# The gate's depthwise convolution of a Branchformer layer, forward and gradient: from diagonal products on TensorE to products and sums on VectorE

## The chip, the core and the metric

The kernel runs on one core of one Trainium2 chip. Its engines work side by side and wait for each other by semaphores: PE (TensorE, matmuls into PSUM), DVE (VectorE), ACT (ScalarE), POOL (GpSimd), and SP (SyncE), which issues most of the DMAs. The metric is the device time of one execution in microseconds. Before the change it is 1294.91 us, the median of three runs (1287.72, 1295.05, 1294.91).

## What is computed

The reference is a layer of the Branchformer kind, forward and all gradients, for x of 2 x 4000 tokens of 144 channels, in bf16. The part that matters here is the local branch ("gate"), and its gradient:

```python
h = _gelu(jnp.einsum('btd,de->bte', xc, w_mlp_in))
u, g = (h[..., :D].copy(), h[..., D:].copy())
g = _layernorm(g, axis=-1)
gp = jnp.pad(g, ((0, 0), (pad, pad), (0, 0)))
gc = jnp.zeros_like(g)
for i in range(K):
    gc = gc + gp[:, i:i + T, :] * dw_csgu[i][None, None, :]
loc = jnp.einsum('btd,de->bte', u * gc, w_mlp_out)
```

So `gc` is a convolution over time with 5 taps, each channel by itself (depthwise). The gradient with regard to `g` is the same convolution with the taps in reverse order, applied to the gradient of `gc`; the gradient with regard to the taps `dw_csgu` (5 x 144) is a sum over all tokens of products of `g`, shifted by the tap, with the gradient of `gc`. Beside this branch stands attention over 4000 tokens (scores, softmax, values, and their gradients), and behind both a merging convolution with products.

## The kernel before: how the work is tiled and ordered

**Layout.** The 4000 tokens of a batch lie on 125 partitions (`PB`) with 32 consecutive tokens (`NB`) each: token t is partition t // 32, block t % 32. A shift in time by one token is therefore another block of the same partition; only at the first and last blocks does it come from the neighbouring partition (a DMA shifted by one partition).

**The attention loop** (`phase_att`, L1201) takes 64 steps, one for each block of 125 tokens of both batches, with a few more to drain. In each step PE computes four pairs of score and gradient products into PSUM (`quad`, L1273), DVE takes the scores out with a minimum (`S_min`, L1298), ACT takes the exponentials (L1304), the gradient's products are multiplied with the probabilities (`PdP`, L1310: an ACT copy and a DVE product in SBUF, or a direct DVE product from PSUM, L1312, for the last of the four), SP issues DMA transposes of the result, and PE multiplies the results with tokens (`Y_half`, `Z_half`, `X_group`). DVE adds the groups of `X` to an accumulator (L1416); the first group of each block is copied (L1414).

**The local units** (`local_units`, L546) are spread over the steps 2 to 26 for batch 0 and 34 to 60 for batch 1. They come in 16 units for a batch, of two blocks (`G2`) each. For unit g: two matmuls for the hidden layer (L590), the gelu and its derivative on ACT, DVE and POOL (L592 to L651), statistics (L610), the product of `go` with the merging weights (`dug_unit`, L618), the normalized gate (`e_gn`, L632, POOL) and the gradient of `gc` (`e_dgc`, L636, DVE). The last two are written side by side into a tile of a small ring, `gd`, `[125, 2, 2 blocks, 144]`.

**The convolution before** runs on PE. `t_unit` (L653) transposes both halves of a `gd` tile with four matmuls against the identity (channels 0 to 127) and four more for the 16 remaining channels, whose 5 taps are stacked on 80 partitions (`rem`); ACT copies the results (`gT`, `gS`). `gc_unit` (L671) multiplies for each block five shifted transposed tiles with diagonal matrices of the taps (`W.dgf`), and one stacked tile with `W.dgs`: 12 matmuls a unit, whose result ACT copies from PSUM (L678). `dgn_unit` (L686) does the same for the gradient with `W.dgm`, which has one column more: it gives the sum over the channels, which the gradient of the normalization needs. DVE reads this result from PSUM (L696, L700, L708). `dwc_unit` (L728) computes the gradient of the taps on PE, for every second unit: for channels 0 to 127 as products of all channel pairs whose diagonal `Final.dwc` (L1890) takes at the end, for the other 16 with the stacked tile.

**The order.** The program is written as one list, and `Planner.plan` (L927) then orders the instructions of each engine with a list scheduler: it has a cost for each instruction (`cost`, L891), a model of the DMA queue, the tiles' dependencies, and a table of lead times (`LEAD`, L792) that moves groups of instructions ahead or back. Each engine works strictly in that order. A round of the local branch (`round_`, L761) puts the new work of unit n beside the convolution of an older unit o.

**The head.** Before the loop, weights are loaded and prepared (`Head`, L116); PE runs 100 matmuls on zeros (`WARM`, L541; `warm`, L180) that the planner puts wherever PE has nothing else, and `conv` (L285) builds the diagonal matrices on POOL.

## Time and profile before

| | |
|---|---|
| median of three runs | 1294.91 us |
| the profiled execution | 1292.98 us |
| its span, first to last instruction | 1291.2 us |
| PE busy / weight loads | 1257.1 / 1040.6 us |
| DVE, ACT, POOL busy | 1047.1, 788.2, 501.1 us |
| instructions | 39494 |
| DMA | 185.80 MB, 76.7% of 16 engines' span on the main queue |
| granted TensorE clock, mean | 0.991 |

A time line or a group of the profile names the source line, the engine, the operation, output and inputs with their sizes, and the duration. The idle time behind it is that of the engine just before the instruction, with what ended it. Busy times of an engine are the union of its records, so two records that overlap count once. `PEclk` or the seventh figure of a window row is the share of the full TensorE clock that was granted. The record of a short matmul (0.22 us) is its latency; the next one starts much earlier, so what a matmul costs is read from start to start.

### The profile page before, as it was taken

To read this page: it belongs to the slowest core of one execution; us is meant where nothing else is said; L and a number is where in the kernel's file an instruction comes from. 1 tells how busy PE (TensorE), PEld (TensorE's weight loads), DVE (VectorE), ACT (ScalarE), POOL (GpSimd) and SP (SyncE) were. 2 spreads that over 40 slices of the span, in tenths; PEclk is the share of its full clock that TensorE was granted. 3 is DMA by queue.
4 is the path that set the end of the run, shared out by engine and by line. 5 is a ranking of instruction groups with operands and counts; after the bars stand their busy time and mean duration, and the time that the engine had idled before them with its cause. 6 is when DMAs were issued, how large, how long until landed. Compare 5 with 4: busy or idle time off the path is not lost.

```text
span 1291.2 us, 39494 instructions
## 1 busy us (share of the span) xinstructions
PE 1257.1 (97%) x15974; PEld 1040.6 (81%) x15974; DVE 1047.1 (81%) x2809; ACT 788.2 (61%) x1291; POOL 501.1 (39%) x976
## 2 busy tenths in 40 slices
PE   8999999999999999899899999999999999899898
PEld 6578888888888887777678888888888888799897
DVE  6589888988888887898888888899889887666925
ACT  4776666666665666556656666667566665435561
POOL 6265335444443434232444434444443433132410
PEclk8899999999999999999999999999999999999999
DMA  4477888888888888889898898887778788959611
GB/s 126 94 141 136 155 144 152 143 145 150 137 151 142 145 143 162 158 145 174 168 155 148 133 149 135 151 137 146 137 142 154 136 155 167 188 123 208 186 44 50
DMA packets 628829, 185.80 MB, mean 144 GB/s; under 512 B 604215, under 2 KB 623065, under 8 KB 628625
## 3 DMA queue, kind: packets, MB, share of 16 engines
q1 hardware_dynamic: 627506, 181.88, 76.7%
q8 instruction: 125, 2.05, 0.6%
q0 software_dynamic: 592, 1.18, 0.3%
q14 instruction: 58, 0.48, 0.1%
q10 hardware_dynamic: 548, 0.21, 0.1%
HBM read 22.96 MB, written 16.69 MB: 31 GB/s over the span
## 4 chain that ended last, share of the span: by engine, by line
PE 83%; DMA 6%; DVE 3%; ACT 3%; SPq 2%; POOL 1%; issue 1%; ACTq 0%; POOLq 0%
PE X L1410 20%; PE ps L1276 15%; PE yz L1363 10%; PE yz L1325 9%; PE ps L1283 7%; DMA ST<-Sbuf 2%; PE po L1783 2%; DMA PT<-Pbuf 2%; PE pd L625 1%; PE pd L692 1%; PE pc L677 1%; PE pj L1249 1%; PE Hps L1698 1%; PE pt L1265 1%; PE pw L737 1%; DVE Pbuf L1298 1%
## 5 line engine op out<-in xcount | busy, mean ns | idle before, releaser
L1298 DVE TENSOR_SCALAR_CACHE_REDUCE Pbuf<-ps 125x1000 bf16<-125x1000 f32 x256 | 306.4, 1197 | 93.9 <-PE ps L1283 90.0
L1304 ACT ACTIVATE Pbuf<-Pbuf,nm 125x1000 bf16<-125x1000 bf16 x256 | 278.6, 1130 | 91.1 <-DVE nm L1300 90.7
L1410 PE MATMUL X<-QBs,Sbuf 125*125 125x144 bf16 x2048 | 298.8, 229 | 0.8 <-DVE acc L1414 0.4
L1410 PE MATMUL X<-QBs,Pbuf 125*125 125x144 bf16 x2048 | 292.3, 226 | 0.0
L1410 PEld LDWEIGHTS <-Sbuf 125*125 125x125 bf16 x2048 | 259.3, 137 | 26.0 <-issue 25.8
L1314 ACT CAST Sbuf<-ps 125x1000 bf16<-125x1000 f32 x190 | 188.7, 993 | 132.4 <-PE ps L1283 131.1
L1276 PE MATMUL ps<-xaT_m,qt 128*125 128x500 bf16 x1024 | 263.7, 378 | 2.9 <-DVE Pbuf L1298 2.1
L1410 PEld LDWEIGHTS <-Pbuf 125*125 125x125 bf16 x2048 | 260.6, 137 | 0.9 <-issue 0.9
L1416 DVE TENSOR_TENSOR acc<-X,acc 125x432 f32<-125x432 f32 (+1 forms) x373 | 200.5, 549 | 25.2 <-PE X L1410 22.3
L1363 PE MATMUL yz<-xa_aug,ST 125*125 125x144 bf16 x2048 | 150.6, 228 | 6.1 <-DMA ST<-Sbuf 4.8
L1276 PEld LDWEIGHTS <-qt 128*125 128x125 bf16 x1024 | 121.5, 137 | 42.8 <-issue 4.6
L1325 PE MATMUL yz<-xa_aug,PT 125*125 125x145 bf16 x2048 | 146.1, 228 | 6.5 <-DMA PT<-Pbuf 6.5
L1363 PEld LDWEIGHTS <-ST 125*125 125x125 bf16 x2048 | 139.4, 138 | 9.9 <-DMA ST<-Sbuf 6.1
L1325 PEld LDWEIGHTS <-PT 125*125 125x125 bf16 x2048 | 137.4, 137 | 9.6 <-DMA PT<-Pbuf 7.4
L1316 DVE TENSOR_TENSOR Sbuf<-Sbuf,Pbuf 125x1024 bf16<-125x1024 bf16 x190 | 134.6, 710 | 3.5 <-ACT Sbuf L1314 3.1
L1283 PEld LDWEIGHTS <-qt 16*125 16x125 bf16 x1024 | 36.6, 128 | 101.2 <-issue 101.2
L1283 PE MATMUL ps<-XR,qt 16*125 16x500 bf16 x1016 | 111.1, 420 | 0.0
L1343 POOL TENSOR_SCALAR QBs<-qb,rl 125x144 bf16<-125x144 bf16 x64 | 27.0, 422 | 180.5 <-DVE rl L1331 151.1
L1312 DVE TENSOR_TENSOR Sbuf<-ps,Pbuf 125x1000 bf16<-125x1000 f32 x66 | 78.8, 1194 | 6.7 <-PE ps L1283 6.2
L720 POOL TENSOR_TENSOR A_dwc<-l_fl,A_dwc 128x512 f32<-128x512 f32 (+2 forms) x48 | 37.0, 771 | 78.8 <-ACT l_fl L719 78.8
L1267 ACT COPY qt<-pt 128x500 bf16<-128x500 bf16 x62 | 35.9, 578 | 45.5 <-PE pt L1265 44.8
L595 POOL TENSOR_SCALAR l_a<-l_sq 125x576 bf16<-125x576 bf16 x32 | 22.5, 702 | 101.6 <-ACT l_sq L593 101.3
(576 smaller groups left out, 2411.3 us busy)
## 6 DMA issues: line engine op xcount, KB each, us to landing
Yn_d<-yn SPq DMA_DIRECT2D x64, 35.2 KB
Zn_d<-zn SPq DMA_DIRECT2D x64, 35.2 KB
ug_d<-ugr SPq DMA_DIRECT2D x32, 70.3 KB
PT<-Pbuf SPq DMA_TRANSPOSE x126
ST<-Sbuf SPq DMA_TRANSPOSE x126
Yg<-Yn_d SPq DMA_DIRECT2D x8, 252.0 KB
go_h<-in_grad_out_dram SPq DMA_DIRECT2D x8, 252.0 KB
Yg<-ug_d SPq DMA_DIRECT2D x8, 252.0 KB
```

The source lines that it names most:

```text
L720: nc.gpsimd.tensor_tensor(acc, fl[0:rows, 0:n], acc, op=ALU.add)
L1276: mm = nc.tensor.matmul(pp[r // 2][:, r % 2, 0:CH], QT[i][:, 3 * h, :], bs(i)[0].xaT_m[:, c * CH:(c + 1) * CH], start=True, stop=False)
L1283: nc.tensor.matmul(pp[r // 2][:, r % 2, 0:CH], QT[i][rs, 1 + (q // 2 + h) % 2, :], xr, start=False, stop=True)
L1298: nc.vector.tensor_scalar(pv(Pbuf, i % NPB, c2), src, -1.0, 3.0e38, op0=ALU.mult, op1=ALU.min, accum_out=NM[i][:, c2:c2 + 1])
L1304: nc.scalar.activation(v, v, ACT.Exp, bias=NM[i][:, 4:5], scale=-1.0)
L1312: nc.vector.tensor_tensor(pv(Sbuf, i % NDB, c2), src, pv(Pbuf, i % NPB, c2), op=ALU.mult)
L1314: nc.scalar.copy(pv(Sbuf, i % NDB, c2), src)
L1316: nc.vector.tensor_tensor(sc, sc, pchunk(i % NPB, c2), op=ALU.mult)
L1325: nc.tensor.matmul(Y, PT[0:PB, j, 0:PB], S.xa_aug[:, j, 0:D + 1], start=(j == 0), stop=(j == NB - 1))
L1363: nc.tensor.matmul(Z, ST[0:PB, j, 0:PB], S.xa_aug[:, j, 0:D], start=(j == 0), stop=(j == NB - 1))
L1410: nc.tensor.matmul(X[:, jj, :], l, r, start=(n_ == 0), stop=(n_ == len(ops) - 1))
L1416: nc.vector.tensor_tensor(av, X[:, 0:nj, :], av, op=ALU.add)
```

## The change

The taps are no longer applied on PE. The two halves (normalized gate, gradient of `gc`) of all units are written into one ring `[125, 2, 16 blocks, 144]`: 12 blocks are in turn, and the first four are copied behind the twelfth, so that any window of five blocks is contiguous. The halves of the batch's edges wait in `hold` and are copied into the ring after round 13. The taps lie in SBUF on every partition (`W.Wc`, by one broadcast DMA; the second half is the reverse order, by a POOL copy). DVE multiplies, for each block, five blocks x 144 channels with five taps in one instruction, and sums the five products with three instructions a unit:

```diff
-    def t_unit(c, g):
-        pt = ps_w.tile([128, 8, 128], BF, tag="w")
...
+    def taps(g, a):
+        p = (G2 * g) % 12
+        for bi in range(G2):
+            nc.vector.tensor_tensor(prod[:, bi].rearrange("p a b -> p (a b)"), ring[:, a, p + bi:p + bi + 5, :].rearrange("p a b -> p (a b)"), W.Wc[0:PB, a, :], op=ALU.mult)
+        nc.vector.tensor_tensor(t2[:], prod[:, :, 0:2, :], prod[:, :, 2:4, :], op=ALU.add)
+        nc.vector.tensor_tensor(t1[:], t2[:, :, 0, :], t2[:, :, 1, :], op=ALU.add)
 
     def gc_unit(g):
-        pc = ps_w.tile([PB, G2, D], F32, tag="w")
-        for bi in range(G2):
-            i = G2 * g + bi
-            nc.tensor.matmul(pc[:, bi, :], gS[g % 2][:, bi, :], W.dgs[:, 0, 0:D], start=True, stop=False)
-            for kk in range(5):
-                nc.tensor.matmul(pc[:, bi, 0:128], col(0, i + kk), W.dgf[:, kk, :], start=False, stop=(kk == 4))
-        nc.scalar.copy(gc[:], pc[:])
+        taps(g, 0)
+        nc.vector.tensor_tensor(gc[:], t1[:], prod[:, :, 4, :], op=ALU.add)
...
     def dgn_unit(g):
-        pd = ps_w.tile([PB, G2, D + 1], F32, tag="w")
...
+        taps(g, 1)
+        rs, t = rsr[slot(g)], gd(g)
+        s1 = sm.tile([PB, G2], F32, tag="s1")
         s2 = sm.tile([PB, G2], F32, tag="s2")
         for bi in range(G2):
-            nc.vector.scalar_tensor_tensor(gc[:, bi, :], pd[:, bi, 1:D + 1], -1.0 / D, t[:, 0, bi, :], op0=ALU.mult, op1=ALU.mult, accum_out=s2[:, bi:bi + 1])
+            nc.vector.scalar_tensor_tensor(dgn[:, bi, :], t1[:, bi, :], 1.0, prod[:, bi, 4, :], op0=ALU.mult, op1=ALU.add, accum_out=s1[:, bi:bi + 1])
+        for bi in range(G2):
+            nc.vector.scalar_tensor_tensor(gc[:, bi, :], dgn[:, bi, :], -1.0 / D, t[:, 0, bi, :], op0=ALU.mult, op1=ALU.mult, accum_out=s2[:, bi:bi + 1])
```

The ring's copies replace the small copies of the remainder channels, and the gradient of the 16 remaining taps is a product of 16 rows with 80 columns:

```diff
-        nc.gpsimd.tensor_copy(rem[:, :, G2 + G2 * g:2 * G2 + G2 * g, :], t[:, :, :, 128:D])
+        p = (G2 * g + 2) % 12
+        if p < 4 and 0 < g < NG2 - 1:
+            nc.gpsimd.tensor_copy(ring[:, :, 12 + p:14 + p, :], t)
...
+    def e_hold():
+        nc.gpsimd.tensor_copy(ring[:, :, 8:12, :], hold[:])
...
-                nc.tensor.matmul(pw[0:80, 128:128 + D], rem[:, 0, i:i + 5, :].rearrange("p a b -> p (a b)"), t[:, 1, bi, :], start=False, stop=last, skip_group_check=True)
+                nc.tensor.matmul(pw[0:DR, 128:208], t[:, 128:D], ring[:, 0, p:p + 5, 128:D], start=False, stop=last, skip_group_check=True)
```

The diagonal matrices and their preparation in the head are gone (ten tiny DMAs on SP among it), and `Final.dwc` writes its output with one DMA in place of six. Three further edits go with it:

```diff
-WARM = 100
+WARM = 36
...
+        lead = next(g for g, G in enumerate(groups) if G["e"] == "PE" and G["t"].startswith("pt"))
+        for g, G in enumerate(groups):
+            if G["x"] < 0:
+                after[g].add(lead)
...
-            nc.vector.tensor_copy(av, X[:, 0:nj, :])
+            nc.scalar.copy(av, X[:, 0:nj, :])
...
-                PdP(s - 1, q ^ 1, ps[1], q == 3)
+                PdP(s - 1, q ^ 1, ps[1], False)
```

The warming matmuls (`x` below zero) are fewer and may only be placed after PE's first transposes of tokens; the first copies into the accumulator go to ACT; and the fourth gradient product of a step takes the way of the other three (ACT copy, then a DVE product in SBUF) instead of a direct DVE product from PSUM. Last, the planner's costs, its waits between engines and its model of the DMA queue are replaced, and the table `LEAD` is new in all its entries, now with separate values for steps 26 to 38 ("B") and from step 60 on ("E").

More of the change, by code (lines that the diff above doesn't have):

```diff
@@ new lines, in cost, with moved @@
+        return d, d + 0.06
+    def moved(self, ins):
+        a = ins.outs[0]
+        n = self.count(a)
+        if type(ins).__name__ == "InstDmaTransposeAnt":
+            return (2 if n > 1500 else 3), n / 2048.0
+        b = n * (4.0 if a.bass_ap.tensor.dtype == F32 else 2.0) * a.bass_ap.ap[0][1]
+        src = next((q for q in ins.ins if hasattr(q, "bass_ap")), None)
+        far = src is not None and getattr(src.bass_ap.tensor, "tag_meta", None) is None
+        return (1 if far else 0), b / 200e3
```

246 lines of the change are left out of this document (108 added, 138 removed), and 42 rows, old and new, of the table LEAD.

## The prediction

> **What bounds the kernel now.** I read the page first (busy times, then the chain that ended last), then busy time by stage, and then single instructions on the time line.
>
> ```profile
> PE 1257.1 (97%) x15974; PEld 1040.6 (81%) x15974; DVE 1047.1 (81%) x2809; ACT 788.2 (61%) x1291; POOL 501.1 (39%) x976
> ...
> PE 83%; DMA 6%; DVE 3%; ACT 3%; SPq 2%; POOL 1%; issue 1%; ACTq 0%; POOLq 0%
> ```
>
> PE is busy almost throughout and 83% of the chain lies on it. A busy PE need not be a full one, so the stages matter: columns are the window, its length, then busy time and instructions of PE, weight loads, DVE, ACT, POOL, then granted clock, DMA share and GB/s. 128 to 550 (window A) and 690 to 1115 (window B) are the stretches in which batch 0 and batch 1 do their local (gate) work beside attention; 75 to 100 is the stretch where DVE is densest.
>
> ```profile
> 128.00:550.00 422.00, 416.10 (x5303) 342.17 (x5300) 361.69 (x949) 268.95 (x426) 174.16 (x341) 1.00 0.85 148
> 690.00:1115.00 425.00, 424.03 (x5372) 347.25 (x5370) 365.25 (x914) 268.67 (x421) 169.92 (x326) 1.00 0.83 147
> ...
> 75.00:100.00 25.00, 23.96 (x288) 19.11 (x287) 23.59 (x63) 19.85 (x34) 18.36 (x34) 1.00 0.80 144
> ```
>
> PE is busy 98.6% of A and 99.8% of B. DVE is the second engine: 361.7 of 422 and 365.3 of 425, some 86%. So there are 60 us of free DVE in each window, and the change takes PE work and puts it there. The question is whether it fits.
>
> **What leaves PE.** One unit (two blocks of 125 tokens) has a transposing step and two sets of 12 matmuls.
>
> ```profile
> 301.33 0.23 PE L690 MATMUL pd<-dgs,gS 80*125 80x145 bf16 x1
> ...
> 302.04 0.23 PE L1410 MATMUL X<-QBs,Sbuf 125*125 125x144 bf16 x1
> ...
> 309.21 0.38 PE L658 MATMUL pt<-ident,gd 125*128 125x125 bf16 x4
> ...
> 309.65 0.23 PE L1410 MATMUL X<-QBs,Sbuf 125*125 125x144 bf16 x1
> ```
>
> PE issues without a gap here, so the price is start to start, not the 0.23 us of a record: the gradient's 12 matmuls take 302.04 - 301.33 = 0.71 us, the 8 transposes 309.65 - 309.21 = 0.44. The forward set has the same 12 matmuls less one column each; I take 0.70. One unit: 1.85 us; 32 units: 59 us. The gradient of the 16 remaining channels moves 80 columns in place of 144 (32 units x 2 matmuls at under 0.03 us: under 2 us). The number of units in each window, by the forward set's tile (PE, then the ACT copy x15):
>
> ```profile
> 128.00:550.00 422.00, 13.28 (x180) 6.03 (x15) 1.00 0.85 148
> ...
> 690.00:1150.00 460.00, 13.27 (x180) 5.98 (x15) 1.00 0.82 146
> ```
>
> 15 x 1.85 = 28 us in each window (the last two units lie outside). If nothing else held, A would take 394 and B 397.
>
> **What DVE gets.** Eleven instructions for a unit: four products of 720 bf16 elements, two sums of 576, three sums of 288 (the last replaces ACT's copy of `pc`), and two passes of 144 with an accumulator. The trace has no 720, so I bound it by the rows on both sides. Windowed groups (mean ns before the last bar) and time line:
>
> ```profile
> L1316 DVE TENSOR_TENSOR Sbuf<-Sbuf,Pbuf 125x1024 bf16<-125x1024 bf16 x72 | 50.7, 706 | 1.7 <-ACT Sbuf L1314 1.7
> L1312 DVE TENSOR_TENSOR Sbuf<-ps,Pbuf 125x1000 bf16<-125x1000 f32 x24 | 28.7, 1194 | 0.0
> ...
> L709 DVE TENSOR_TENSOR dhr<-l_dd,gpr 125x576 bf16<-125x576 bf16 x16 | 7.2, 450 | 0.0
> ...
> L680 DVE TENSOR_TENSOR ugr<-ur,l_gc 125x288 bf16<-125x288 bf16 x15 | 5.7, 378 | 0.5 <-ACT l_gc L678 0.4
> ```
>
> ```profile
> 302.50 0.31 DVE L696 SCALAR_TENSOR_TENSOR l_gc<-pd,gd 125x144 bf16<-125x144 f32 x1
> ...
> 302.73 0.69 DVE L1316 TENSOR_TENSOR Sbuf<-Sbuf,Pbuf 125x1024 bf16<-125x1024 bf16 x1
> 303.34 0.16 DVE L630 SCALAR_TENSOR_TENSOR rsr<-mv,rsr 125x2 f32<-125x2 f32 x1
> ...
> 309.23 0.46 DVE L709 TENSOR_TENSOR dhr<-l_dd,gpr 125x576 bf16<-125x576 bf16 x1
> 309.60 0.36 DVE L1367 SCALAR_TENSOR_TENSOR zn<-yz,rl,ty 125x144 bf16<-125x144 f32 x1
> ...
> 312.94 1.20 DVE L1312 TENSOR_TENSOR Sbuf<-ps,Pbuf 125x1000 bf16<-125x1000 f32 x1
> 314.05 0.15 DVE L1300 TENSOR_REDUCE nm<-nm 125x1 f32<-125x4 f32 x1
> ```
>
> ```profile
> 166.53 0.31 DVE L680 TENSOR_TENSOR ugr<-ur,l_gc 125x288 bf16<-125x288 bf16 x1
> 166.76 0.77 DVE L684 TENSOR_TENSOR l_dd<-dugr,l_gc 125x288 bf16<-125x288 bf16 x1
> 167.45 0.44 DVE L604 TENSOR_TENSOR l_hg<-l_q,l_hs 125x576 bf16<-125x576 bf16 x1
> ```
>
> The next instruction starts some 0.08 us before the record ends. Start to start: 1024 elements 0.61, 576 elements 0.37, 288 elements 0.23, a pass with accumulator 0.23. Between 576 and 1024, 720 comes to 0.37 + 144/448 x 0.24 = 0.45. A unit: 4 x 0.45 + 2 x 0.37 + 3 x 0.23 + 2 x 0.23 = 3.7 us. That is the low end. The high end takes whole records with the waits that they hold: 4 x 0.53 + 2 x 0.45 + 3 x 0.38 + 2 x 0.31 = 4.8 us. For 32 units: 118 to 153 us.
>
> DVE also gives work back: in each step one direct product from PSUM (L1312, x24 in A) becomes an ACT copy and a product in SBUF, 1.11 (314.05 - 312.94) down to 0.61: 0.5 us in each of A's 24 steps, 12 us, and by the same count 13 in B with its 26. The two existing PSUM readers of the gradient (L696, L708) read SBUF bf16 instead; I take no difference. The first copies into `acc` go to ACT; they lie in the first steps of each batch, ahead of the windows, and I take zero.
>
> A then asks DVE for 361.7 - 12 + 15 x (3.7 to 4.8) = 405 to 422 us; B for 365.3 - 13 + 56 to 72 = 408 to 424. Both are above PE's 394 and 397: **the bound changes hands**, and what is gained is not the 28 us but the distance to DVE's new load, -17 to 0 in each window, by these records. Two corrections nearly cancel: the exposed 0.08 us tails go when the next instruction is always there (some 60 idle gaps and the small-tile chains; I estimate 10 us less), and an engine that bounds still idles a little (A's PE 1.4%: 6 us more). Middle of the range, less 4: A 409, B 412: **-13 and -13**.
>
> **What holds these numbers up.** (1) The lock. At 166.76 a 288-element product took 0.77 where the others take 0.3. POOL shows why:
>
> ```profile
> 166.56 0.81 POOL L603 TENSOR_SCALAR l_q<-l_th 125x576 bf16<-125x576 bf16 x1
> ```
>
> POOL's instruction ends at 167.37, and the product's last 0.3 us begin about there: DVE stood until POOL was through. All eleven new instructions read two operands from SBUF, and POOL is busy 174 of A's 422 us. L680's mean of 378 against 0.31 undisturbed makes 0.07 a hit; eleven a unit are 0.8 us, which is most of the distance from 3.7 to 4.8. The Trainium skill, page "SBUF — State Buffer", section "Who interferes with whom", says that a VectorE instruction with two SBUF inputs and a GpSimd one that reads SBUF exclude each other for a whole instruction; this row agrees, and by that rule the sum would lie at the 4.8 end.
> (2) Waits. The products of unit g need unit g+1's tile in the ring, made by POOL (normalized gate) and DVE one round earlier, a round being over a step of 17.6 us (422/24): hidden. If that cover is gone, every minimum over the scores (L1298) is queued behind the waiting product on DVE, and PE waits for its PSUM. The sums depend on the products right before them; other DVE work can stand between, and if it does not, each costs about a tail (six a unit, 0.5 us, inside 3.7 to 4.8).
> (3) ACT: one more copy a step and the first `acc` copies, against three copies a unit that go (`pc` and the two of the transposes). At 61% on the page it has the room; priced at nothing.
> (4) POOL: 32 small remainder copies go, at most five ring copies a batch come, the two `hold` and ring DMAs on SP stay, ten tiny weight DMAs on SP's queue become one broadcast, six output DMAs become one: nothing, since POOL is busy 39% and none of these is on the chain.
> (5) The order. Lead times and costs of the planner change everywhere. PE is idle for 34 us in all (1291 - 1257, the head included), so a better order can bring at most some of that, and a worse one may cost as much: zero taken, +-10 kept.
>
> **The head.** 100 warming matmuls become 36, and those may only come after PE's first transposes of tokens.
>
> ```profile
> 10.52 6.07 PE L187 MATMUL warm<-wz 128*128 128x256 bf16 x54
> 16.43 1.09 PE L410 MATMUL pt<-ident,xa_aug 125*128 125x125 bf16 x8
> ...
> 20.10 0.28 PE L1432 MATMUL pj<-RW,R 128*125 128x144 bf16 x1 [2.14 <-DVE R L415]
> ```
>
> ```profile
> 16.00:20.00 4.00, 1.82 (x22) 1.29 (x19) 3.97 (x21) 0.99 (x1) 4.00 (x5) 1.00 0.48 182
> 20.00:24.00 4.00, 2.89 (x25) 1.90 (x25) 3.83 (x18) 3.66 (x10) 3.78 (x6) 0.81 0.12 33
> 24.00:28.00 4.00, 4.00 (x25) 2.50 (x24) 1.95 (x7) 2.36 (x5) 4.00 (x12) 0.50 0.15 39
> ...
> 36.00:40.00 4.00, 4.00 (x22) 2.53 (x21) 1.36 (x3) 1.63 (x5) 3.91 (x13) 0.50 0.02 0
> ```
>
> All 54 warm matmuls are done before 16.43; then PE idles 2.14 us and more, the granted clock drops to 0.50 and stays there from 24 to 40 though PE is busy every microsecond of it. Filling those gaps instead can keep or restore the clock: 16 us at half clock are 8 us at full, so -8 at best. At worst 36 matmuls of 0.11 us (6.07/54), twice that at half clock, stand in PE's way: 4 to 8 us against gaps of over 3, so +5. I take -3. The page "TensorE: Matmul & The Clock Gate" of the Trainium skill (section "What's actually happening") has the clock up after one busy window of about 3.4 us; the rows above, 16 us busy at 0.50, do not agree, and by the rule this term would be -8 and the sum 1260. I give that rule 3 in 10 for this term; it shifts the forecast within its range.
>
> **Sum.** 1291.2 - 13 - 13 - 3 = 1262 of span, and 1.8 us around it (the profiled execution took 1292.98): 1264. That execution stands 1.9 us below the median of 1294.91, so against the median it is 1266; I take 1265.
>
> **Rivals.**
> *PE stays the bound.* DVE hides the products wholly in its 60 us of idle time. For: 3.7 a unit and gone tails make 361.7 - 12 + 56 - 10 = 395, just PE's 394. Against: 75 to 100 is DVE's densest stretch and reaches 23.59 of 25. Time: 1293 - 28 - 28 - 5 = 1232.
> *Nothing gained.* DVE asks 422 and 424, the high ends, with no idle time: 1293 - 0 - 1 - 0, about 1292. For: L680's mean includes just such waits. Against: 0.08 us of each record is free. This is the case that the rule of the Trainium skill on the shared ports would make of the lock.
> *Slower.* The lock: one mechanism, DVE's products standing behind POOL's reads, in A and B. It decides from the point where DVE's load at its densest share (23.59/25 = 94.4%) passes the present time: 0.944 x 422 = 398 = 361.7 - 12 + 15 d, d = 3.3 a unit. By that share alone the change is slower from the start, with d = 4.3 A takes 414/0.944 = 438, +16, B 417/0.944 = 441, +16, together about 1323. For: that no stretch shows DVE denser. Against: DVE is not the bound in that stretch, PE is busy 23.96 of the same 25 us, and PE shows 99.8% where it does bound.
>
> **How the numbers follow.** Forecast, a part of PE's gain: 0.45, own range 1246 to 1281. PE stays the bound (1232): 0.17. Nothing gained (1292): 0.21. Slower (1323): 0.17. A measurement of this kernel can tell about 1%, 13 us, from no change. Faster than 1282: 0.45 + 0.17 and a little from the third case's lower edge, 0.63; within 1%: 0.21; slower: 0.16. The range leaves out half of the slower case and the best of the PE case: 1234 to 1304.
>
> **What would show it.** Right: DVE over 95% busy in both windows and PE down to about 95%, PE's waits naming DVE (`Pbuf` L1298 ahead of `ps`), the products near 0.53 us by record, steps of about 17.0 us in A. Head: clock 1.00 from about 24 on. Wrong: PE still at 98% or more with a shorter window (first rival); products of 0.7 us and more with POOL instructions ending in them (slower); a time at which the windows are unchanged and only the head moved.

## The result, and the profile after

The changed kernel takes 1278.05 us, the median of 8 runs (1274.99 to 1282.49), against 1291.21 for the kernel before (8 runs, 1285.42 to 1298.56): a ratio of 0.989 with a 95% interval of 0.987 to 0.991. That is 13 us faster, inside the forecast's own range of 1246 to 1281, and a little under half of the 29 us that its sum held. The reasons behind the sum hold only in part. The profiled execution of the kernel after took 1277.55 us, with a span of 1275.7.

The page of the kernel after, busy times and chain:

```profile
PE 1208.7 (95%) x14868; PEld 980.9 (77%) x14868; DVE 1140.9 (89%) x3209; ACT 805.5 (63%) x1276; POOL 531.8 (42%) x932
...
DVE 51%; PE 32%; issue 6%; ACT 3%; DMA 3%; POOL 3%; SPq 0%; DVEq 0%; ACTq 0%; POOLq 0%
```

PE had 83% of the chain and has 32% now; DVE went from 3% to 51%. The two windows of the prediction, A and B, in the kernel after (columns as there: PE, weight loads, DVE, ACT, POOL, clock, DMA share, GB/s):

```profile
128.00:550.00 422.00, 400.46 (x4808) 318.43 (x4807) 414.99 (x1159) 269.21 (x399) 198.43 (x340) 1.00 0.75 148
690.00:1115.00 425.00, 408.13 (x4889) 324.49 (x4887) 409.72 (x1090) 269.74 (x397) 177.45 (x311) 1.00 0.75 149
```

DVE is busy 98.3% and 96.4%, PE 94.9% and 96.0%: the bound changed hands, as forecast. So do the waits (what waited, for what, us in all, times, longest), first of the kernel before, then of the kernel after:

```profile
DVE Pbuf L1298 <- PE ps L1283: 90.0, 129, 3.8
```

```profile
DVE Pbuf L1302 <- PE ps L1287: 26.6, 39, 1.7
PE ps L1280 <- DVE Pbuf L1302: 15.6, 30, 1.4
```

DVE waited 90 us for scores and waits 27; PE now waits 16 us for DVE's minimum over the scores to free its PSUM (2 before).

**Where the time came from.** Fixed windows do not compare two kernels of different length. A better ruler is an instruction that each step has once: the final reduce of the minimum over the scores. With steps counted from 0, this is its record at step 3 of the kernel before and then of the kernel after:

```profile
89.53 0.15 DVE L1300 TENSOR_REDUCE nm<-nm 125x1 f32<-125x4 f32 x1
```

```profile
85.15 0.15 DVE L1304 TENSOR_REDUCE nm<-nm 125x1 f32<-125x4 f32 x1
```

Steps 3 to 26 and 37 to 61 are the *dense* stretches, which hold the 16 local units of batch 0 and of batch 1; 26 to 37 lies *between* them and has little local work (the first instructions of some three units of batch 1, and almost nothing of the convolution: one forward set of 12 matmuls and its transposes before, two products after). Read that way for all kernels of this study (us, from the profiled executions; the names are explained with the experiments):

| kernel | to step 3 | 3 to 26 (dense) | 26 to 37 (between) | 37 to 61 (dense) | 61 to 63 | from 63 | span |
|---|---|---|---|---|---|---|---|
| before | 89.5 | 395.8 | 193.5 | 407.0 | 29.5 | 175.9 | 1291.2 |
| **after** | **85.2** | **405.5** | **172.5** | **413.5** | **29.7** | **169.4** | **1275.7** |
| after less before | -4.3 | +9.7 | -21.0 | +6.5 | +0.2 | -6.5 | -15.5 |
| pe_conv_new_plan | 88.8 | 400.7 | 196.1 | 426.1 | 28.8 | 183.9 | 1324.3 |
| dve_conv_old_plan | 83.3 | 420.0 | 191.4 | 426.7 | 29.3 | 169.6 | 1320.3 |
| before_no_table | 98.3 | 402.3 | 195.0 | 414.7 | 29.0 | 176.6 | 1315.8 |
| pe_conv_no_table | 87.5 | 405.7 | 190.7 | 412.9 | 30.9 | 175.6 | 1303.2 |
| after_no_table | 86.0 | 405.7 | 180.2 | 416.6 | 30.4 | 177.8 | 1296.7 |
| old_head_edit | 86.3 | 395.8 | 193.9 | 407.0 | 30.6 | 173.3 | 1286.8 |
| new_old_head | 90.4 | 404.5 | 180.0 | 413.6 | 28.9 | 169.0 | 1286.4 |
| new_dve_direct | 86.4 | 416.0 | 189.0 | 428.0 | 29.9 | 174.6 | 1323.8 |
| new_twice_sums | 85.2 | 421.0 | 176.6 | 427.1 | 30.0 | 169.9 | 1309.7 |
| new_less_sums | 84.7 | 398.5 | 178.2 | 410.4 | 28.5 | 171.5 | 1271.8 |
| one_tap | 85.5 | 383.4 | 179.8 | 399.2 | 27.1 | 179.4 | 1254.5 |
| new_la_act | 86.0 | 400.8 | 176.7 | 413.1 | 29.6 | 170.4 | 1276.6 |

The two stretches in which the convolution lies, and from which the forecast took its 26 us, became **longer**, by 9.7 and 6.5 us. The gain came between the batches, at the head and at the end. (The ruler has a play of a few us: products that follow the scores late can fall on the other side of a mark. Steps 3 to 26 of the kernel after hold 33 more matmuls of `X` and `yz` and 24 more of `pw` than before, steps 37 to 61 68 more of `X` and `yz`: some 4 us of PE's work each, at 0.06 from start to start, which lay between the batches and at the end before. Free of that play, steps 3 to 61 together take 991.5 us where they took 996.3.)

The same three stretches (3 to 26, 26 to 37, 37 to 61) as windows of the kernel before, then of the kernel after:

```profile
89.53:485.30 395.77, 395.34 (x5042) 325.74 (x5041) 345.10 (x907) 257.63 (x415) 172.41 (x330) 1.00 0.84 146
485.30:678.80 193.50, 180.71 (x2207) 144.58 (x2205) 161.49 (x402) 114.72 (x164) 68.45 (x141) 0.99 0.88 160
678.80:1085.80 407.00, 406.81 (x5179) 334.37 (x5178) 352.27 (x899) 260.90 (x413) 169.84 (x326) 1.00 0.82 144
```

```profile
85.15:490.62 405.47, 383.91 (x4582) 305.03 (x4580) 400.94 (x1106) 258.07 (x394) 194.92 (x323) 1.00 0.72 142
490.62:663.13 172.51, 167.72 (x2052) 133.97 (x2051) 149.36 (x379) 122.54 (x175) 65.08 (x129) 1.00 0.90 175
663.13:1076.60 413.47, 397.38 (x4767) 316.76 (x4765) 407.39 (x1113) 262.73 (x394) 183.36 (x318) 1.00 0.73 145
```

In the dense stretches PE was busy 99.9% and 100.0% and DVE is now busy 98.9% and 98.5%. DVE's load there rose by 55.8 and 55.1 us, but before it had only 50.7 and 54.7 us free. Between the batches PE is busy 13.0 us less and idle 8.0 us less (12.8 to 4.8).

### The profile page after: what moved, and what is told of

Its sections match the earlier page's. It is cut to its first block, busy times and chain, and to the rows that moved or that the text cites. A ratio compares the mean times of both kernels' runs of the same rounds, so it can differ in the third digit from the quotient of the medians.

```text
span 1275.7 us, 37546 instructions
## 1 busy us (share of the span) xinstructions
PE 1208.7 (95%) x14868; PEld 980.9 (77%) x14868; DVE 1140.9 (89%) x3209; ACT 805.5 (63%) x1276; POOL 531.8 (42%) x932
## 4 chain that ended last, share of the span: by engine, by line
DVE 51%; PE 32%; issue 6%; ACT 3%; DMA 3%; POOL 3%; SPq 0%; DVEq 0%; ACTq 0%; POOLq 0%
DVE Pbuf L1302 12%; DVE acc L1420 7%; DVE Sbuf L1320 7%; PE X L1414 7%; PE ps L1280 5%; DVE l_prod L638 4%; PE yz L1367 3%; PE yz L1329 3%; PE po L1787 3%; PE Hps L1702 2%; PE ps L1287 2%; DVE l_t L639 2%; DMA PT<-Pbuf 2%; ACT Pbuf L1308 1%; DVE l_dgn L658 1%
## 5 line engine op out<-in xcount | busy, mean ns | idle before, releaser
L1318 ACT CAST Sbuf<-ps 125x1000 bf16<-125x1000 f32 x252 | 250.4, 994 | 195.2 <-PE ps L1287 191.9
L1302 DVE TENSOR_SCALAR_CACHE_REDUCE Pbuf<-ps 125x1000 bf16<-125x1000 f32 x256 | 304.9, 1192 | 28.5 <-PE ps L1287 26.6
L1308 ACT ACTIVATE Pbuf<-Pbuf,nm 125x1000 bf16<-125x1000 bf16 x256 | 283.4, 1137 | 47.4 <-DVE nm L1304 47.2
L1320 DVE TENSOR_TENSOR Sbuf<-Sbuf,Pbuf 125x1024 bf16<-125x1024 bf16 x252 | 185.6, 737 | 3.4 <-ACT Pbuf L1308 2.2
L1280 PEld LDWEIGHTS <-qt 128*125 128x125 bf16 x1024 | 124.3, 136 | 64.6 <-issue 23.6
L1329 PE MATMUL yz<-xa_aug,PT 125*125 125x145 bf16 x2048 | 150.4, 228 | 9.0 <-DVE zn L1371 6.7
L1329 PEld LDWEIGHTS <-PT 125*125 125x125 bf16 x2048 | 138.7, 137 | 21.1 <-issue 16.7
L1347 POOL TENSOR_SCALAR QBs<-qb,rl 125x144 bf16<-125x144 bf16 x64 | 30.9, 483 | 200.0 <-DVE rl L1335 196.5
L638 DVE TENSOR_TENSOR l_prod<-ring,Wc 125x720 bf16<-125x720 bf16 x128 | 71.2, 574 | 0.2 <-POOL ring L611 0.2
L1263 POOL COPY qr<-qb 125x64 bf16<-125x64 bf16 x124 | 37.9, 336 | 69.7 <-ACT qb L1255 69.6
L683 POOL TENSOR_TENSOR A_dwc<-l_fl,A_dwc 128x512 f32<-128x512 f32 (+2 forms) x48 | 38.3, 798 | 55.8 <-ACT l_fl L682 55.8
L666 POOL TENSOR_SCALAR l_w<-ring,nc,c 125x144 f32<-125x144 bf16 x60 | 34.5, 580 | 45.8 <-DVE nc L662 43.2
```

Source lines behind the costliest of these rows:

```text
L638: nc.vector.tensor_tensor(prod[:, bi].rearrange("p a b -> p (a b)"), ring[:, a, p + bi:p + bi + 5, :].rearrange("p a b -> p (a b)"), W.Wc[ ...
L683: nc.gpsimd.tensor_tensor(acc, fl[0:rows, 0:n], acc, op=ALU.add)
L1280: mm = nc.tensor.matmul(pp[r // 2][:, r % 2, 0:CH], QT[i][:, 3 * h, :], bs(i)[0].xaT_m[:, c * CH:(c + 1) * CH], start=True, stop=False)
L1302: nc.vector.tensor_scalar(pv(Pbuf, i % NPB, c2), src, -1.0, 3.0e38, op0=ALU.mult, op1=ALU.min, accum_out=NM[i][:, c2:c2 + 1])
L1308: nc.scalar.activation(v, v, ACT.Exp, bias=NM[i][:, 4:5], scale=-1.0)
L1318: nc.scalar.copy(pv(Sbuf, i % NDB, c2), src)
```

## The experiments

Twelve kernels were run. Ratios are to the kernel before, with 95% intervals.

**Does the move, or what goes with it, change the time? The four corners.** The change moves the convolution and brings a new order (costs, table) and small edits. In every kernel below the planner lists the order anew for the edit, so each difference holds the edit and what the new list makes of it. `pe_conv_new_plan` is the kernel before, convolution on PE, with everything else of the change:

```diff
-WARM = 100
+WARM = 36
...
     LEAD = {
-        "H DVE raw 1008": -246, "H POOL ident 128": 38, "H POOL Wi 288": 113, "H POOL xa_aug 32": 32, "H POOL go_q 576": -13, "H SP go_q 576": -144,
+        "H DVE wz 256": 28, "H DVE raw 1008": -18, "H ACT raw 144": -101, "H DVE lnst 6": 114, "H DVE lnve 8": -79, "H PE hps 0": 146,
...
-            nc.vector.tensor_copy(av, X[:, 0:nj, :])
+            nc.scalar.copy(av, X[:, 0:nj, :])
...
-                PdP(s - 1, q ^ 1, ps[1], q == 3)
+                PdP(s - 1, q ^ 1, ps[1], False)
```

> The kernel before, with the convolution still on TensorE, but with all else that the change brought: the new planner, its table, the head with 36 warming matmuls behind the first transposes, the first copies into acc and the fourth gradient product by way of ACT. Theory (moving the convolution is worth nothing, because VectorE becomes the bound; the head, the stretch between the batches and the end brought the 13 us): 1270 to 1282 us, as fast as the change or faster, VectorE near 85% busy in the two stretches of local work, and these not longer than before (396 and 407 us from the 3rd to the 26th and from the 37th to the 61st score minimum). Rival (the move is worth some 15 us and other edits cost): 1285 to 1300.

Measured 1321.87 us, ratio 1.021 [1.017, 1.025]: slower than both kernels, and above every case that was named. `dve_conv_old_plan` is the opposite corner, the kernel after with the planner, costs and table of before (and without the rule that holds the warming matmuls back):

```diff
     LEAD = {
-        "H DVE wz 256": 28, "H DVE raw 1008": -18, "H ACT raw 144": -101, "H DVE lnst 6": 114, "H DVE lnve 8": -79, "H PE hps 0": 146,
+        "H DVE raw 1008": -246, "H POOL ident 128": 38, "H POOL Wi 288": 113, "H POOL xa_aug 32": 32, "H POOL go_q 576": -13, "H SP go_q 576": -144,
...
-        lead = next(g for g, G in enumerate(groups) if G["e"] == "PE" and G["t"].startswith("pt"))
-        for g, G in enumerate(groups):
-            if G["x"] < 0:
-                after[g].add(lead)
```

> The kernel after with the planner, the costs and the lead table of the kernel before, so with the convolution on VectorE in an order that was listed for the convolution on TensorE. It is the fourth corner beside before (1291), after (1278) and pe_conv_new_plan (1322: the convolution on TensorE, the order listed for VectorE). Theory: a lead table belongs to its kernel, and a foreign one costs some 15 to 45 us on either side; the move is worth what it is worth only together with its own table: 1295 to 1330, steps 26 to 37 over 185 us. Rival 1: the order does not matter for the convolution on VectorE, the move itself is the gain: 1272 to 1285. Rival 2: the move costs by itself and only the rest of the change pays: 1330 and more, that is, further above 1322 minus 13.

Measured 1328.72, ratio 1.027 [1.023, 1.031], steps 26 to 37 at 191.4: the theory. With the planner and table of the other kernel the time is 30 and 50 us above that of `before` and after, more than the change is worth, so these two corners say nothing of the move itself. Three kernels with an empty table say more (`pe_conv_no_table` is `pe_conv_new_plan` with this edit):

```diff
-    LEAD = {
-        "H DVE wz 256": 28, "H DVE raw 1008": -18, "H ACT raw 144": -101, "H DVE lnst 6": 114, "H DVE lnve 8": -79, "H PE hps 0": 146,
...
-    }
+    LEAD = {}
```

> The kernel after with an empty lead table: its planner then lists the order from its costs alone, tuned for neither place of the convolution. To be read against pe_conv_no_table, which differs in the place of the convolution alone. Theory, the move itself is worth something in any order: this one is 10 to 40 us below pe_conv_no_table, and 15 to 60 above after (1278). Rival, what tells before and after apart is the tuning of the table: this one is within 10 us of pe_conv_no_table or above it.

> The kernel pe_conv_new_plan (the convolution on TensorE, all other edits of the change made) with an empty lead table. Theory, the move itself is worth something: 10 to 40 us above after_no_table; and, as the table listed for VectorE does not suit this kernel, no more than 20 us above its 1322, or even below it. Rival, the move is worth nothing and the table is all: within 10 us of after_no_table or below it.

> The kernel before with an empty lead table, to be read beside after_no_table (1300.5) and pe_conv_no_table (1305.2). Theory, a table that was listed for its kernel is worth some 15 to 25 us on either side (22 in after), so the whole change is worth about the same with and without tables: 1306 to 1320, 10 to 20 above after_no_table. Rival, before had little from its table and the gain of the change is that of its table: 1292 to 1303, within 5 us of after_no_table. If it is over 1325, the costs that the planner of before works with are poor by themselves, and the new costs are part of the gain.

Measured: `before_no_table` 1317.64, ratio 1.022 [1.019, 1.025], the theory; `pe_conv_no_table` 1305.17, 1.009 [1.006, 1.011], and `after_no_table` 1300.50, 1.006 [1.003, 1.008], for both the rival. The order's tables are worth 27 us in before and 22 in after. Without them the whole change is worth 17 us, of which 12.5 come from the new costs, the head and the ACT edits, and 4.7 from the move. The theory asked for 10 us at least from the move. The two intervals overlap, but they share the noise of `before`; the runs themselves do not (1298.47 to 1302.30 against 1302.33 to 1305.48), so in this pair the 4.7 us are a small difference and not noise. It is one listed order on each side, and whether the place of the convolution or the list makes it is not shown. Stage by stage it is two effects of opposite sign. Steps 3 to 26 and 26 to 37 with the convolution on PE (`pe_conv_no_table`), then on DVE (`after_no_table`):

```profile
87.48:493.20 405.72, 398.68 (x5052) 327.17 (x5050) 333.90 (x894) 278.67 (x439) 173.17 (x327) 1.00 0.82 142
493.20:683.86 190.66, 176.79 (x2174) 141.56 (x2173) 150.84 (x391) 127.39 (x185) 68.97 (x142) 1.00 0.89 160
```

```profile
85.97:491.68 405.71, 382.16 (x4540) 303.52 (x4538) 400.25 (x1100) 255.31 (x389) 187.92 (x317) 1.00 0.71 142
491.68:671.90 180.22, 175.73 (x2140) 141.88 (x2139) 151.47 (x399) 124.96 (x179) 68.59 (x137) 0.98 0.86 170
```

The dense stretch has the same length to 0.01 us, once with PE 98.3% busy and once with DVE 98.7% busy; 37 to 61 is 3.7 us longer with DVE. The gain of this pair, 10.5 us, lies between the batches, where there is almost no convolution. What PE waits for there, before and after, and then with the empty table on PE and on DVE:

```profile
PE yz L1325 <- DMA PT<-Pbuf: 4.8, 4, 2.5
PE yz L1363 <- DMA ST<-Sbuf: 3.3, 3, 1.8
...
PE pt L495 <- DMA pgo_h<-in_grad_out_dram: 0.8, 2, 0.7
```

```profile
PE yz L1367 <- ACT ty L1345: 2.9, 6, 0.8
...
PE yz L1329 <- DMA PT<-Pbuf: 0.3, 1, 0.3
...
PE pt L473 <- DMA pgo_h<-in_grad_out_dram: 0.2, 1, 0.2
```

```profile
PE yz L1341 <- DMA PT<-Pbuf: 6.6, 5, 2.4
PE pt L495 <- DMA pgo_h<-in_grad_out_dram: 2.6, 2, 1.5
PE yz L1379 <- DMA ST<-Sbuf: 2.0, 3, 1.3
```

```profile
PE yz L1341 <- DMA ST<-Sbuf: 0.6, 1, 0.6
```

With the convolution on PE, PE waits 8.9 and 11.2 us for DMA transposes and loads; with it on DVE 0.5 and 0.6. That makes up nearly the whole of the empty-table difference, and 8 of the 21 us between before and after; the other 13 us are PE's busy time (155 fewer matmuls in the stretch: 51 of `X`, 36 of `yz` and 28 of `pw`, some 7 us of work that lies in other stretches now, and 40 of the local units' transposes and products). Why the transposes come in time once the convolution has left PE was not settled: the share of the DMA engines hardly differs (0.89 against 0.86). The table of stretches shows that 172.5 us belong to this one listed order: in each of the eight variants of the kernel after, from `dve_conv_old_plan` to `new_la_act`, the stretch takes 4 to 19 us more, although most of their edits change little in it.

**Is DVE the bound in the dense stretches? The slope.** The sum of 576 elements is issued twice (`new_twice_sums`), or left out with products 2 and 3 computed but unused (`new_less_sums`):

```diff
-        nc.vector.tensor_tensor(t2[:], prod[:, :, 0:2, :], prod[:, :, 2:4, :], op=ALU.add)
+        for _ in range(2):
+            nc.vector.tensor_tensor(t2[:], prod[:, :, 0:2, :], prod[:, :, 2:4, :], op=ALU.add)
```

```diff
-        nc.vector.tensor_tensor(t2[:], prod[:, :, 0:2, :], prod[:, :, 2:4, :], op=ALU.add)
-        nc.vector.tensor_tensor(t1[:], t2[:, :, 0, :], t2[:, :, 1, :], op=ALU.add)
+        nc.vector.tensor_tensor(t1[:], prod[:, :, 0, :], prod[:, :, 1, :], op=ALU.add)
```

> The kernel after with the sum of 576 elements issued twice in both calls of the taps, with the same result. 64 instructions of 0.37 to 0.50 us are added to VectorE: 24 to 32 us. Theory, VectorE sets the pace: 1298 to 1312. Rival, free time on VectorE takes half or more of it: 1280 to 1292. Beside new_less_sums it gives the slope on both sides: a bound that changes hands just here would show a full cost on this side and less than half a gain on the other.

> The kernel after without the sum of 576 elements in both calls of the taps: l_t is product 0 plus product 1 alone, so products 2 and 3 are computed and left out of the convolution and of its gradient. 64 instructions of 0.50 us by record (0.37 start to start) leave VectorE: 24 to 32 us, nothing else changes in count. Theory, VectorE sets the pace in both local stretches: nearly all of it is gained, 1245 to 1258, VectorE still over 95% busy from 128 to 550 us. Rival, TensorE and VectorE wait for one another in turn and neither load is the bound: less than half of it, 1266 to 1280.

Measured 1311.13 (1.014 [1.011, 1.016]) and 1272.56 (0.985 [0.982, 0.987]): +33.1 and -5.5 us against the kernel after. The theory holds on the one side, its rival on the other. Steps 3 to 26 with the sum twice, with the sum left out, and with one tap (next):

```profile
85.15:506.17 421.02, 386.31 (x4555) 306.27 (x4552) 412.93 (x1135) 257.08 (x393) 203.87 (x321) 0.99 0.69 137
```

```profile
84.73:483.26 398.53, 380.69 (x4552) 303.69 (x4550) 389.79 (x1067) 256.31 (x391) 186.45 (x318) 1.00 0.73 144
```

```profile
85.50:468.90 383.40, 375.12 (x4513) 299.18 (x4511) 358.44 (x1038) 257.05 (x390) 177.95 (x317) 1.00 0.74 150
```

DVE's busy time goes up by 12.0 and the stretch by 15.5: full price and more. It goes down by 11.2 and the stretch by 6.9, the second dense stretch by 3.1, and 5.6 of that are lost between the batches. The 32 sums change DVE's busy time by 0.35 to 0.38 us each, near the price from start to start and not the 0.50 of a record (an estimate: in the two kernels 7 and 3 other instructions left the stretch as well). How much of PE's relief would come out if DVE were lighter shows `one_tap`, which computes the convolution and its gradient from their last tap alone, added to itself so that the last sum of each call stays:

```diff
-            nc.vector.tensor_tensor(prod[:, bi].rearrange("p a b -> p (a b)"), ring[:, a, p + bi:p + bi + 5, :].rearrange("p a b -> p (a b)"), W.Wc[0:PB, a, :], op=ALU.mult)
-        nc.vector.tensor_tensor(t2[:], prod[:, :, 0:2, :], prod[:, :, 2:4, :], op=ALU.add)
-        nc.vector.tensor_tensor(t1[:], t2[:, :, 0, :], t2[:, :, 1, :], op=ALU.add)
+            nc.vector.tensor_tensor(prod[:, bi, 4, :], ring[:, a, p + bi + 4, :], W.Wc[0:PB, a, 4 * D:5 * D], op=ALU.mult)
...
-        nc.vector.tensor_tensor(gc[:], t1[:], prod[:, :, 4, :], op=ALU.add)
+        nc.vector.tensor_tensor(gc[:], prod[:, :, 4, :], prod[:, :, 4, :], op=ALU.add)
...
```

> The kernel after with the convolution and its gradient cut to their last tap: products of 144 elements in place of 720, no sums of 576 and 288 elements; the other four taps are left out of the result. VectorE loses some 3.2 us in each of 32 units by the records of after (4 x 0.574 less about 4 x 0.2, 2 x 0.502, 2 x 0.343), about 100 us in all; TensorE's work and everything else stay. Theory, VectorE's load is what eats TensorE's relief: with it gone the relief of 1.85 us a unit comes out, steps 3 to 26 at 366 to 380 and 37 to 61 at 377 to 390 (396 and 407 before, 405 and 413 after), time 1205 to 1240. Rival, the listed order makes the engines wait for each other whatever VectorE's load: both stretches stay over 390, time 1250 to 1275.

Measured 1253.59 (0.969 [0.966, 0.972]). The time lies in the rival's range; of the stretches, 383.4 lies between the two cases and 399.2 in the rival's. They take 12.4 and 7.8 us less than before and not 28; DVE is at 93.5% in the first, PE at 97.8%. With 42.5 us of DVE's load gone from it, PE is the busier engine again, but the stretch takes more than the 366 us (395.8 less 16 x 1.85) that start-to-start prices give; the next section shows where the rest goes.

**What DVE gave back.** `new_dve_direct` is the kernel after with the fourth product read directly from PSUM and the first copies into `acc` on DVE, as before:

```diff
-            nc.scalar.copy(av, X[:, 0:nj, :])
+            nc.vector.tensor_copy(av, X[:, 0:nj, :])
...
-                PdP(s - 1, q ^ 1, ps[1], False)
+                PdP(s - 1, q ^ 1, ps[1], q == 3)
```

> The changed kernel with the two ACT edits undone: the fourth gradient product of a step directly from PSUM on VectorE, the first copies into acc on VectorE. That gives VectorE 0.5 us a step back, 25 us over the two stretches of local work. Theory (VectorE is the bound there): 1295 to 1308 us. Rival (VectorE's load is not what sets the time): within 5 us of the change, 1273 to 1283.

Measured 1323.75 (1.023 [1.019, 1.027]), 46 us above the kernel after: the direction of the theory, and more than it. The dense stretches grow by 10.5 and 14.5, near the 12 and 13 that the prediction gave these edits; the stretch between grows by 16.5, where 0.5 us a step make 6. With these products left on DVE, and in an order whose table was made with them on ACT, the move loses; how much of the 46 us is the order was not taken apart.

**The head.** `old_head_edit` is the kernel before with 36 warming matmuls, held behind the first transposes; `new_old_head` is the kernel after with 100 and without that rule, this diff taken back:

```diff
-WARM = 100
+WARM = 36
...
+        lead = next(g for g, G in enumerate(groups) if G["e"] == "PE" and G["t"].startswith("pt"))
+        for g, G in enumerate(groups):
+            if G["x"] < 0:
+                after[g].add(lead)
```

> The kernel before with the head's edit alone: 36 warming matmuls, only behind the first transposes of tokens. Theory (the head gives 8 to 9 us, since the clock stays at full speed from 24 us on): 1280 to 1286 us, the score minimum of step 2 at about 65 us instead of 74. Rival (the head's gain came from the fewer instructions in the head, or is lost behind it): 1288 to 1293.

> The changed kernel with the head's edit undone: 100 warming matmuls wherever TensorE is free. Theory (head worth 8 to 9 us): 1284 to 1289 us, the granted clock at 0.50 between about 24 and 40 us again. Rival (worth nothing): 1276 to 1280.

Measured 1291.70 (0.999 [0.997, 1.002]) and 1287.75 (0.997 [0.994, 0.999]): of the first expectation the rival came true, with step 2 at 70.8 us instead of 65; of the second the time came true, but not its reason, since the clock was not at 0.50 from 24 to 40. The clock from 24 to 44 us in before and in `old_head_edit`, then from 20 to 24 and 24 to 44 in `new_old_head`:

```profile
24.00:44.00 20.00, 20.00 (x112) 11.83 (x111) 9.41 (x19) 9.56 (x22) 10.33 (x34) 0.53 0.05 12
```

```profile
24.00:44.00 20.00, 17.99 (x175) 11.68 (x174) 14.08 (x28) 15.71 (x33) 10.83 (x34) 1.00 0.39 61
```

```profile
20.00:24.00 4.00, 3.54 (x24) 2.68 (x25) 2.68 (x12) 2.79 (x8) 3.58 (x7) 0.57 0.09 26
24.00:44.00 20.00, 18.36 (x181) 11.89 (x181) 13.45 (x27) 15.54 (x31) 6.59 (x16) 1.00 0.36 94
```

The edit lifts the clock from 0.53 to 1.00 and saves 3.2 us up to step 3 in before. In the profiled execution that stays until the end; in the medians nothing of it can be seen. In the kernel after the old head costs 10 us, but not by the clock: step 2 comes at 65.0 as against 65.4, and the loss lies in steps 2 to 3 (5.7) and between the batches (7.5), in the order.

**The lock.** `new_la_act` moves the two scalings `l_a` of each unit from POOL to ACT:

```diff
-            nc.gpsimd.tensor_scalar(a_[:], sq[:], K0 * K1, K0, op0=ALU.mult, op1=ALU.add)
+            nc.scalar.activation(a_[:], sq[:], ACT.Copy, scale=K0 * K1, bias=K0)
...
-        nc.gpsimd.tensor_scalar(a_[:], sq[:], 6 * K0 * K1, 2 * K0, op0=ALU.mult, op1=ALU.add)
+        nc.scalar.activation(a_[:], sq[:], ACT.Copy, scale=6 * K0 * K1, bias=2 * K0)
```

> The kernel after with the two scalings of 576 elements in each unit (l_a, some 46 us of GpSimd in all) moved from GpSimd to ScalarE, with the same formula. Theory, VectorE's instructions with two SBUF inputs stand behind GpSimd's reads, and that is part of why a product of 720 elements takes 0.574 us by record: the products fall to 0.55 or less, the exponentials' products (1024 elements) below 0.72, and the time to 1262 to 1272. Rival, GpSimd's reads cost VectorE next to nothing: records within 2% of those of after, time 1274 to 1284. If ScalarE's added 40 us come between TensorE and its copies, the time rises to 1285 and more with the products' records unchanged or lower.

Measured 1278.21 (0.989 [0.986, 0.992]), no different from the kernel after: the rival's time. DVE's groups over the whole span, after and then `new_la_act` (busy us, mean ns of one):

```profile
L1320 DVE TENSOR_TENSOR Sbuf<-Sbuf,Pbuf 125x1024 bf16<-125x1024 bf16 x252 | 185.6, 737 | 3.4 <-ACT Pbuf L1308 2.2 <-ACT Sbuf L1318 0.8
L638 DVE TENSOR_TENSOR l_prod<-ring,Wc 125x720 bf16<-125x720 bf16 x128 | 71.2, 574 | 0.2 <-POOL ring L611 0.2
L639 DVE TENSOR_TENSOR l_t<-l_prod 125x576 bf16<-125x576 bf16 x64 | 32.2, 502 | 0.1
```

```profile
L1320 DVE TENSOR_TENSOR Sbuf<-Sbuf,Pbuf 125x1024 bf16<-125x1024 bf16 x252 | 178.8, 710 | 7.9 <-ACT Sbuf L1318 4.6 <-ACT Pbuf L1308 2.9
L638 DVE TENSOR_TENSOR l_prod<-ring,Wc 125x720 bf16<-125x720 bf16 x128 | 72.7, 582 | 1.1 <-POOL ring L618 0.6 <-POOL ring L611 0.5
L639 DVE TENSOR_TENSOR l_t<-l_prod 125x576 bf16<-125x576 bf16 x64 | 30.0, 468 | 0.0
```

Two of the three groups get shorter, by 6.8 and 2.2 us in all, the products do not (+1.5): POOL's 46 us of scalings cost DVE some 7.5 us in these groups. In steps 3 to 26 DVE is busy 4.9 us less and the stretch is 4.7 shorter; but the second dense stretch gains only 0.4 and the stretch between loses 4.2, so that nothing is left in the time.

The edit takes 46 of POOL's 532 us away; the trace of the kernel after shows the lock itself. Of its 128 products of 720 elements, the 105 during which no POOL instruction ends take 0.52 us by record and 0.44 from start to start. The other 23 take 0.82, and each of them ends 0.38 to 0.40 us after the POOL instruction that ends during it, whenever the product had started:

```profile
994.45 0.45 POOL L683 TENSOR_TENSOR A_dwc<-l_fl,A_dwc 128x128 f32<-128x128 f32 x1 [1.59 <-ACT l_fl L682]
994.49 0.80 DVE L638 TENSOR_TENSOR l_prod<-ring,Wc 125x720 bf16<-125x720 bf16 x1
```

Counted in this way, against 0.52, 0.44 and 0.68 us undisturbed, the lock adds 6.9 us to the products, 3.7 to 18 of the sums of 576 and 14.1 to 51 of the exponentials' products, 24.8 us in all; 22.2 of these lie in the two dense stretches. (Before, it adds 5.3 us to 35 of the exponentials' products.) That is more than the 16.2 us by which these grew. The scalings end in only 3 of the 23 products; no kernel was run without the other hits.

None of the twelve points to a version of the whole computation that is faster than the kernel after: even leaving out a whole sum brings only 5.5 us, and `new_la_act` brings none.

## Why the prediction was right, and where it was wrong

**The bound changes hands: right.** DVE over 95%, PE near 95%, PE's waits naming DVE's minimum: these three signs are there, and the slope agrees, since more DVE work costs its full price and less brings over half of it in that stretch. The sign of the steps failed: 17.0 us were forecast, and 405.5 / 23 = 17.6 came, against 17.2 before.

**DVE's load: right.** Forecast 405 to 422 and 408 to 424 in A and B, measured 415.0 and 409.7. In steps 3 to 26 DVE gained 55.8 us net; with the 9.6 it gave back (27.5 + 48.7 by records before, 66.6 in one group after) that is 65.4 / 16 = 4.1 us a unit, inside 3.7 to 4.8. The records themselves sum to 5.2, above the high end of 4.8. Steps 3 to 26 (columns as above) of the kernel before, then after:

```profile
L1316 DVE TENSOR_TENSOR Sbuf<-Sbuf,Pbuf 125x1024 bf16<-125x1024 bf16 x69 | 48.7, 707 | 1.7 <-ACT Sbuf L1314 1.7
L1312 DVE TENSOR_TENSOR Sbuf<-ps,Pbuf 125x1000 bf16<-125x1000 f32 x23 | 27.5, 1194 | 0.0
```

```profile
L1320 DVE TENSOR_TENSOR Sbuf<-Sbuf,Pbuf 125x1024 bf16<-125x1024 bf16 x93 | 66.6, 716 | 0.0
L638 DVE TENSOR_TENSOR l_prod<-ring,Wc 125x720 bf16<-125x720 bf16 x64 | 36.4, 586 | 0.2 <-POOL ring L611 0.2
L639 DVE TENSOR_TENSOR l_t<-l_prod 125x576 bf16<-125x576 bf16 x32 | 16.7, 520 | 0.0
...
L658 DVE SCALAR_TENSOR_TENSOR l_dgn<-l_t,l_prod 125x144 bf16<-125x144 bf16 x32 | 11.4, 356 | 0.1
L640 DVE TENSOR_TENSOR l_t<-l_t 125x288 bf16<-125x288 bf16 x32 | 10.7, 335 | 0.0
...
L644 DVE TENSOR_TENSOR l_gc<-l_t,l_prod 125x288 bf16<-125x288 bf16 x16 | 6.3, 391 | 0.0
...
L658 DVE DVE_READ_ACCUMULATOR l_dgn<-l_t,l_prod 125x1 f32 x32 | 2.4, 76 | 0.0
```

The six new groups make 83.9 us; between 5.2 and 4.1 lies the overlap of records: in this stretch the sum of all DVE records exceeds its busy time by 59.7 us before and by 81.4 after, 1.4 us a unit more.

**-13 and -13: the step that failed.** "A then asks DVE for 361.7 - 12 + 15 x (3.7 to 4.8) = 405 to 422 us [...] what is gained is not the 28 us but the distance to DVE's new load" set the load against a window of 422 us. But 64.7 us of A (485.3 to 550) lie between the batches, and that stretch's free DVE time can't take work that stands before step 26. Cut at the units' own stretch, the prediction's numbers say it: 345.1 busy, less 11.5, plus 16 x 3.7 to 4.8, is 393 to 410 in 395.8 us, so -3 to +14; measured 405.5, +9.7. For batch 1: 352.3 - 12 + 59 to 77 is 399 to 417 in 407.0; measured 413.5. The window made free room that was not there, and with it the gain. That the time still fell inside the range is luck: the two stretches from which 26 us were to come lost 16, and what the range was met with came from where the sum held zero.

**PE's relief: the price was right, and another term had the wrong sign.** From start to start, the convolution's matmuls and transposes (`pc`, `pd`, `pt`) take 30.1 us less of steps 3 to 26 in `one_tap` than before, against 29.6 forecast (16 x 1.85). PE's busy time falls by only 20 us (395.3 to 375.1), and the stretch by 12.4. One part of the difference is the gradient of the taps, the term that was to save "under 2 us" by moving 80 columns in place of 144. Its pair of matmuls for a block, before and after:

```profile
153.63 0.22 PE L739 MATMUL pw<-gd,gd 125*128 125x128 bf16 x1
153.69 0.23 PE L740 MATMUL pw<-gd,gd_rem 125*80 125x144 bf16 x1
153.75 0.22 PE L739 MATMUL pw<-gd,gd 125*128 125x128 bf16 x1
```

```profile
200.59 0.23 PE L702 MATMUL pw<-ring 125*128 125x128 bf16 x1
200.75 0.20 PE L704 MATMUL pw<-ring 125*16 125x80 bf16 x1
200.89 0.23 PE L702 MATMUL pw<-ring 125*128 125x128 bf16 x1
```

The pair took 0.12 us and takes 0.30. With weights of 16 columns in place of 80, both its matmuls become slower, by 5.5 us for the 32 blocks of steps 3 to 26 in `one_tap` and 6.1 in the kernel after. In the first pair of rows the weights of L740 begin to load 0.06 us ahead of their product, in the second those of L704 begin with it; why is not shown. All `pw` matmuls together take 7.0 us more in `one_tap` than before (22 more of them lie in the stretch), and the remaining 11 us are longer gaps behind `X`, `yz` and `ps`, among them waits for DVE's minimum (4.4) and for ACT's `ty` (2.5).

**The order: sized wrongly.** "zero taken, +-10 kept" was met by -21.0 us between the batches and -6.5 at the end, work that moved across the marks included. The whole gain stands on them, and on an order whose tables are worth 22 to 27 us. The change gives its table separate values for just the steps 26 to 38; and with the empty table 10.5 us of the 21 remain.

**ACT "priced at nothing", DVE's give-back 12 and 13: right in place, too small in sum.** The dense stretches grow by 10.5 and 14.5 in `new_dve_direct`, but the time by 46 us, with the order's share in it.

**The lock: right in kind, and not an even price.** Undisturbed, the products take 0.52 us by record and 0.44 from start to start, as the prediction's 0.53 and 0.45 had it; their mean of 0.574 is the 23 hits. The exponentials' products went from 0.710 to 0.737 over the whole span. The Trainium skill, page "SBUF — State Buffer", section "Who interferes with whom", has such pairs of VectorE and GpSimd instructions exclude each other for their whole duration. The trace agrees: every hit product ends 0.38 to 0.40 us after POOL's instruction does, nearly a whole product later. The prediction's own row fits too: its 288-element product ends 0.16 us after POOL's record, a shorter rest than the 0.3 that was read there. The slower rival, 0.944 as DVE's densest share, is refuted by 98.9%, though some 10 us of that busy time in steps 3 to 26 is DVE standing behind POOL.

**The head: right size (-3 forecast, -4.3 by step 3), and not by its mechanism alone.** The clock did go to 1.00. But the same edit brings nothing measurable in before, and taking it back in after costs 10 us with the half clock lasting 4 us. The Trainium skill, page "TensorE: Matmul & The Clock Gate", section "What's actually happening", has the clock back after some 3.4 us of sustained work: `new_old_head` agrees, at 0.57 in 20 to 24 and 1.00 after it; before does not, at 0.53 through 20 us in which PE is busy by its records.

**The rivals.** "Nothing gained" is what the dense stretches did. "PE stays the bound" fell with DVE's 98.9% and PE's 94.7% (383.9 of 405.5).

## What to carry to other kernels

Set an engine's new load against the stretch in which the work has to lie, cut at events that both kernels have, and not against a round window: free time outside that stretch is no room. Where two engines are both over 85% busy, moving work from one to the other brought nothing in that stretch here although the bound changed hands; look for what the move does elsewhere. When a program's order is tuned, compare the move with the tuning taken out of both versions, since a table made for the other version can cost more than the change is worth (`pe_conv_new_plan` is 16.7 us slower than with an empty table, and the change is worth 13). And a mean over a group of instructions can hide two prices: sort its records by what ran beside them.

## What was not expected of the hardware

PE ran at about half clock for 20 us in which it was busy without a gap by its records (0.53 granted, 20.00 of 20 us), while in the changed program the same 100 warming matmuls left it there for 4 us only (0.57). A record's mean is no price: the 576-element sum has 0.50 us on record and changes DVE's busy time by 0.35 to 0.38 where it is saturated. And fewer columns cost more: a pair of matmuls with weights of 128 and 80 columns takes 0.12 us from start to start, and one with 128 and 16 columns, which moves less, takes 0.30.
